# Gate and value products as 2x2 blocks with seven block products, and an MLP issued from a table of places

## The chip, the cores and the metric

One core of one Trainium2 chip runs the whole kernel. The metric is device time in microseconds, from launch to end; lower is better.

## The reference

Attention with hashed buckets feeds a gated layer, and that a second one. Cut to what is computed:

```
mask = q_bucket[..., :, None] == k_bucket[..., None, :]     # buckets: signs of q @ proj, k @ proj
scores = where(mask, (q @ k.T) / sqrt(64), -1e9)            # (2, 8, 768, 768)
x = softmax(scores) @ v                                     # -> (1536, 512)
x = (sigmoid(x @ moe_w_gate) * (x @ moe_w_val)) @ moe_w_out # 512 -> 1536 -> 512
h = x @ moe2_w_in                                           # 512 -> 2048
g = where(h >= 1, h, where(h <= -1, 0, (h + 1) ** 2 / 4))
out = g @ moe2_w_out                                        # 2048 -> 512
```

The MLP weights arrive as 64-bit floats, read as int64, and the kernel turns them into fp32 bit by bit.

## The kernel before

**Attention.** Two batches b with four pairs of heads p each give eight pairs q = 0 to 7, about 28 us each. A pair has 12 units (two heads, six row blocks of 128). Per unit TensorE writes the scores (`sc`), VectorE takes the row maximum, ScalarE the exponential `P`; TensorE transposes P into PSUM banks (`pt`), ScalarE copies the high half to f16 (`PT`, L345), VectorE the rest (L348), and TensorE multiplies by v's halves `vh` and `vl` into `O` (L387). GpSimd scales and splits v (L368, L371, L375), prepares q and k of the next pair (L209, L212, L215) and copies reciprocals (`rb`, L536). VectorE reduces v once a pair (L356). The order of all of it is written by hand: a table `AT` gives each step a place in units, `at` adds it to a list, and the sorted list is issued under `manual_schedule`, so that each engine runs its rows in that order.

**Precision.** Every fp32 operand of the MLP is split into a high and a low fp32r half (`split`, `split_w`, `conv_w` with `w_abs`, `w_clamp`, `w_low`, `w_sign` for the 64-bit weights), and a product is three matmuls, high by high, high by low, low by high (`mm3`, L125 to L130). The copies run on ScalarE, the differences on VectorE.

**Gate and value.** For each of 12 chunks of 128 output columns, each batch and each half n of its 768 tokens, `gate_val_n` multiplies four input chunks by the gate weights into one bank `pg`, takes tanh (L150), does the same with the value weights into `pv` and multiplies (L154). `first_weights` converts the first gate and value weights during pairs 1 to 3 in 10 steps, and `gv(0)`, `gv(1)` run the first two products at the end of the attention; `split_x` splits x on GpSimd in the last pair.

**The rest** is in the scheduler's own order from its own pool of eight PSUM banks: `out1` (12 weight chunks into eight accumulators, per batch), then `mlp2` (`act2` and the second output product).

## Time and profile before

| what | us |
| --- | --- |
| median of 3 runs | 825.41 (825.2 to 825.66) |
| span of the profiled execution | 821.7 |
| busy on PE, DVE, ACT, POOL | 804.5, 542.8, 462.3, 119.5 |
| stretch of the attention | 0 to about 249 |

The span runs from the first to the last instruction of the profiled execution on the core; a run's time holds in addition what lies ahead of and behind it. The profiled execution's own time is not recorded beside its span, so the span stands for it and the difference to the median is added. PE is TensorE (PEld its weight loads), DVE VectorE, ACT ScalarE, POOL GpSimd. An engine's busy time counts neither waits nor the issuing of transfers.

### The profile page before, as it was taken

Reading aid. Unit: us, or ns where it says so; the run is one execution under the profiler, and the core shown is the slowest. Engines: PE = TensorE matmul, PEld = TensorE weight load, DVE = VectorE, ACT = ScalarE, POOL = GpSimd, SP = SyncE. Lnnn points to the kernel's source line nnn. Section 1 sums busy time; section 2 is a strip of 40 time slices with the busy share of each in tenths; the row PEclk is TensorE's granted clock in tenths of the full one; section 3 lists DMA queues with packets and bytes.
Section 4 is the critical chain, followed back from the end, with each engine's and each line's share of the span. In section 5 each row is a group of like instructions: output and inputs, shape, how many; then the busy total and the mean of one; then the engine's idle time right before and its main releaser. Section 6 shows DMA issues by size and latency. Waiting matters only on the chain.

```text
span 821.7 us, 13003 instructions
## 1 busy us (share of the span) xinstructions
PE 804.5 (98%) x5098; PEld 736.1 (90%) x5098; DVE 542.8 (66%) x953; ACT 462.3 (56%) x903; POOL 119.5 (15%) x104
## 2 busy tenths in 40 slices
...
PEclk8999999999999999999999999999999999999999
...
GB/s 241 124 120 126 87 107 130 74 133 90 30 2 77 129 73 82 52 52 56 99 155 192 91 77 40 142 178 127 78 1 1 1 1 77 1 1 1 1 0 77
DMA packets 39709, 64.21 MB, mean 78 GB/s; under 512 B 5316, under 2 KB 28228, under 8 KB 39648
## 3 DMA queue, kind: packets, MB, share of 16 engines
...
## 4 chain that ended last, share of the span: by engine, by line
PE 89%; ACT 4%; DVE 3%; DMA 3%; issue 0%; SPq 0%; DVEq 0%
PE sc L301 6%; PE pt L336 6%; PE O L387 6%; PE p L128 5%; PE p L126 5%; PE p L127 5%; PE o L693 5%; PE o L694 5%; PE o L692 5%; PE pg L126 4%; PE pg L128 4%; PE pv L128 4%; PE y L128 4%; PE pg L127 4%; PE y L126 4%; PE pv L127 4%
## 5 line engine op out<-in xcount | busy, mean ns | idle before, releaser
L348 DVE SCALAR_TENSOR_TENSOR PT<-pt,PT 128x512 f16<-128x512 f32 x144 | 95.5, 685 | 19.7 <-ACT PT L345 17.9
L309 DVE TENSOR_REDUCE st<-sc 128x1 f32<-128x768 f32 x96 | 90.9, 948 | 5.4 <-PE sc L301 5.1
L313 ACT ACTIVATE P<-sc,st 128x768 f32<-128x768 f32 x96 | 86.9, 905 | 13.0 <-DVE st L309 12.8
L345 ACT ACTIVATE PT<-pt 128x512 f16<-128x512 f32 x144 | 81.7, 593 | 21.1 <-PE pt L336 20.6
L128 PE MATMUL p<-yh,wl_i 128*128 128x384 f32 x256 | 85.9, 336 | 0.0
L126 PE MATMUL p<-yh,wh_i 128*128 128x384 f32 x256 | 85.8, 335 | 0.0
L127 PE MATMUL p<-yl,wh_i 128*128 128x384 f32 x256 | 85.7, 335 | 0.0
L336 PE MATMUL pt<-ident,P 128*128 128x128 f32 x576 | 80.4, 277 | 4.8 <-DVE PT L348 3.5
L336 PEld LDWEIGHTS pt<-ident,P 128*128 128x128 f32 x576 | 66.0, 141 | 15.8 <-DVE PT L348 8.0
L694 PE MATMUL o<-wh_o,gl 128*128 128x512 f32 x192 | 75.3, 392 | 0.0
L693 PE MATMUL o<-wl_o,gh 128*128 128x512 f32 x192 | 75.2, 392 | 0.0
L692 PE MATMUL o<-wh_o,gh 128*128 128x512 f32 x192 | 74.7, 389 | 0.0
L676 DVE SCALAR_TENSOR_TENSOR g<-p,t 128x384 f32<-128x384 f32 x64 | 35.5, 555 | 48.3 <-ACT t L674 48.3
L154 DVE SCALAR_TENSOR_TENSOR h<-sg,pv 128x384 f32<-128x384 f32 x48 | 26.4, 551 | 50.4 <-PE pv L128 50.3
L150 ACT ACTIVATE sg<-pg 128x384 f32<-128x384 f32 x48 | 23.4, 488 | 63.4 <-PE pg L128 63.1
L673 ACT ACTIVATE t<-p,cst 128x384 f32<-128x384 f32 x64 | 36.7, 573 | 37.0 <-PE p L128 36.8
L677 ACT ACTIVATE gh<-g 128x384 fp32r<-128x384 f32 x64 | 33.6, 525 | 41.2 <-DVE g L676 41.1
L678 DVE TENSOR_TENSOR gl<-g,gh 128x384 fp32r<-128x384 f32 x64 | 35.7, 557 | 31.5 <-ACT gh L677 31.5
L387 PE MATMUL O<-PT,vh 128*64 128x256 f16 x576 | 54.8, 278 | 0.5 <-DVE xr L394 0.5
L126 PEld LDWEIGHTS p<-yh,wh_i 128*128 128x128 f32 x256 | 48.1, 188 | 1.1
L127 PEld LDWEIGHTS p<-yl,wh_i 128*128 128x128 f32 x256 | 48.1, 188 | 1.1
L116 DVE TENSOR_TENSOR wl_o<-w_o,wh_o 128x512 fp32r<-128x512 f32 x56 | 38.6, 689 | 15.0 <-ACT wh_o L115 15.0
(265 smaller groups left out, 2022.7 us busy)
## 6 DMA issues: line engine op xcount, KB each, us to landing
...
```

The costliest lines, as they stand in the source:

```text
L126: nc.tensor.matmul(ps, lhsT=wh, rhs=rh, start=first, stop=False)
L127: nc.tensor.matmul(ps, lhsT=wh, rhs=rl, start=False, stop=False)
L128: nc.tensor.matmul(ps, lhsT=wl, rhs=rh, start=False, stop=last)
L309: nc.vector.tensor_reduce(out=self.st[:, 0, self.c:self.c + 1], in_=self.sc[:, :, 0:HN], op=ALU.max, axis=AX.XY, negate=True)
L313: nc.scalar.activation(out=self.P, in_=self.sc[:, :, 0:HN], func=AF.Exp, bias=self.st[:, 0, self.c:self.c + 1], scale=1.0, accum_out=self. ...
L336: nc.tensor.transpose(self.ps[m][:, j, :], un[2 * self.n + e].P[:, a, c:c + 128], ident)
L345: nc.scalar.activation(out=self.part(0, m), in_=self.ps[m], func=AF.Copy, scale=PSCALE)
L348: nc.vector.scalar_tensor_tensor(out=self.part(1, m), in0=self.ps[m], scalar=PSCALE, in1=self.part(0, m), op0=ALU.mult, op1=ALU.subtract)
L387: nc.tensor.matmul(O_ps[r, 0:GN], lhsT=vv[m][:, e, i * D:(i + 1) * D], rhs=PT[:, l, e * NI + i, :], start=(s == 0), stop=(s == len(steps) ...
L692: nc.tensor.matmul(oacc[i], lhsT=gh[:, ts], rhs=wh, start=(fc == 0), stop=False)
L693: nc.tensor.matmul(oacc[i], lhsT=gh[:, ts], rhs=wl, start=False, stop=False)
L694: nc.tensor.matmul(oacc[i], lhsT=gl[:, ts], rhs=wh, start=False, stop=(fc == F2 - 1))
```

## The change

The weight chunks j and j + 6 form two rows of blocks, the four input chunks two block columns of two, and the two token halves the two block columns of x. In place of the eight block products, each of 2 x 3 matmuls, seven are made (`SEQ`), on sums and differences of blocks: S1 to S4 of the weights (`a_sum`), T1 to T4 of x (`b_sum`). A `Quad` does this for one chunk pair of gate or value (`t` = g0 to g5, v0 to v5) and one batch: 24 quads. A partial result that belongs to two outputs is copied from its PSUM bank to another by ScalarE (`seed`: a to b, b to c, b to d), and the next product adds to the copy; the one of bank e goes to SBUF (`keep5`) and VectorE adds it (`sum`). Banks b, c, d come in turn from the attention's pool, whose first four turns begin with a small matmul of zeros (`qbank`). The x sums and splits of batch 0 go to GpSimd in pairs 4 to 7, `first_weights` has 20 steps in pairs 1 to 5, and quad 0 (`tail`) runs at the end of the attention. From there on all MLP work is issued from one list of places under `manual_schedule`, with one PSUM pool throughout.

```diff
+    SEQ = (("A11", "B11", "a"), ("S1", "T1", "e"), ("S2", "T2", "b"), ("A12", "B21", "a"), ("S3", "T3", "b"), ("S4", "B22", "c"), ("A22", "T4", "d"))
...
-        nc.gpsimd.dma_start(code_f, code_d)
+        nc.sync.dma_start(code_f, code_d)
...
-        return keep.tile([128, S], F32R, tag="qk", bufs=16, name=name)
+        return keep.tile([128, S], dt, tag="qk", bufs=26, name=name)
...
+    def b_sum(eng, b, name, cs=slice(0, 2)):
+        x, y = {"T1": ("B12", "B11"), "T2": ("B22", "T1"), "T3": ("B22", "B12"), "T4": ("B21", "T2")}[name]
+        xsub(eng, BO[b][name][:, cs], b_src(b, x)[:, cs], b_src(b, y)[:, cs])
...
+    def a_conv(t, m):
+        if m < 2:
+            (w_range, w_shift)[m](WO[t]["wt"].bitcast(U32))
+        else:
+            w, (low, high) = a_half(t, m % 2)
+            w_low(w, low) if m < 4 else w_sign(w, high)
+
+    def a_sum(eng, t, m, q2=False):
...
+        o, x, y, op = ((s1, a21, a22, ALU.add), (s2, s1, a11, ALU.subtract), (s3, a11, a21, ALU.subtract), (s4, a12, s2, ALU.subtract))[m]
+        eng.tensor_tensor(out=o, in0=x, in1=y, op=op)
...
+        def keep5(self):
+            self.p5 = self.tmp(f"p5_{self.t}_{self.b}")
+            nc.scalar.activation(out=self.p5, in_=self.K["e"], func=AF.Copy)
+
+        def P(self, i):
+            an, bn, g = SEQ[i]
+            first = i < 2
+            ps = self.new(g) if first else self.K[g]
...
+            for c in range(2):
+                cs = slice(c * 128, (c + 1) * 128)
+                mm3(ps, wh[:, cs], wl[:, cs], rh[:, c], rl[:, c], first and c == 0, c == 1, skip_group_check=True)
+
+        def seed(self, m):
+            src = self.K["abb"[m]]
+            nc.scalar.activation(out=self.new("bcd"[m]), in_=src, func=AF.Copy)
...
+        def sum(self, g):
+
+            d = self.dst(g)
+            if g in "bc":
+                x = self.tmp(f"x{g}_{self.t}_{self.b}") if self.val else d
+                nc.vector.tensor_tensor(out=x, in0=self.K[g], in1=self.p5, op=ALU.add)
+            else:
+                x = self.K[g]
+            if self.val:
+                self.glu(d, x)
...
-    def gate_val_n(b, n, ws, hr, bank, sgt, nm, late=None):
...
+    def qbank(k, g):
+
+        if g in "ae":
...
+            return pairs[g][:, k % 2, 0:HN]
+        t = bank(f"q{g}_{k}", next(ring))[:, 0:HN]
+        if next(turn) < 4:
+            nc.tensor.matmul(t, lhsT=code[:, 0, 0, :], rhs=bt, start=True, stop=True, skip_group_check=True)
+        return t
...
             def first_weights():
...
+                for t in ("g0", "v0"):
+                    for h in range(2):
+                        a_abs(t, h)
+                        yield
+                    for m in range(6):
+                        a_conv(t, m)
+                        yield
+                    a_load({"g0": "v0", "v0": "g1"}[t])
+                    if t == "g0":
+                        for m in range(4):
+                            a_sum(nc.gpsimd, t, m)
+                        a_hi(t, "a")
+                        yield
+                        a_lo(t, "a")
+                        for m in range(2):
+                            a_hi(t, "s", m)
+                            yield
+                            a_lo(t, "s", m)
...
-            for i in range(10):
+            for i in range(20):
                 at(2.2 + 1.2 * (i % 4), 0, 1 + i // 4, next, fw, None)
...
+            x0 = ("T1", "hT1", "hB11", "lB11", "T2", "lT1", "hT2", "T4", "lT2", "T3", "hT3", "lT3", "hT4", "lT4", "hB21", "lB21", "hB22", "lB22")
...
+            place = [(4, 1.0 + 1.3 * i) for i in range(2)] + [(5, 2.0 + 2.1 * i) for i in range(4)] + [(6, 2.0 + 2.1 * i) for i in range(4)] + [(7, 0.5 + 1.2 * i) for i in range(8)]
+            for op, (q, t) in zip(x0, place):
+                at(t, 0, q, x_op, 0, op)
...
-            gv(1)
+            x_op(1, "T2", C1, V)
...
+            tail("P", 4)
...
+    for k in range(1, 2 * NT):
+        s0 = 7 * k
+        for i in range(7):
+            on(s0 + i, q_op, k, "P", i)
+        for m, d in enumerate((0.98, 2.98, 4.98)):
+            on(s0 + d, q_op, k, "seed", m)
+        on(s0 + 1.99, q_op, k, "keep5")
+        for g, d in (("a", 3.99), ("b", 4.99), ("c", 5.99), ("d", 6.99)):
+            on(s0 + d, q_op, k, "sum", g)
+            on(s0 + d + (0.5 if g in "bc" else 0.0), q_op, k, "act", g)
...
+        for m, d in enumerate((0.1, 0.9, 1.7, 2.4, 3.0, 3.6)):
+            on(base + d, a_conv, n, m)
...
+        for m, d in enumerate((8.05, 9.05)):
+            on(base + d, a_hi, n, "s", m, True)
+            on(base + d + 1.0, a_lo, n, "s", m, True)
...
-    for b in range(B):
-        out1(b)
-    for b in range(B):
-        mlp2(b)
+    with tc.manual_schedule():
+        for _, _, fn, args, kw in sorted(prog, key=lambda x: x[:2]):
+            fn(*args, **kw)
```

The order of ScalarE in the second quad (batch 1) of a gate chunk pair, here g4: `qb`, `qc`, `qd` are the seeds, `hs` the high halves of the next value weight sums, `wt` the weight after that, `h1` the gate, `qa` to `qe` the banks. After the change (rows that repeat a tanh left out):

```order
L257 ACTIVATE qb_17_5004<-qa_3678 128x384
L217 ACTIVATE hs_v4_5012<-ws_v4_4964 128x512
L243 ACTIVATE p5_g4_1_5014<-qe_3688 128x384
L217 ACTIVATE hs_v4_5012<-ws_v4_4964 128x512
L257 ACTIVATE qc_17_5025<-qb_17_5004 128x384
L140 ACTIVATE wt_g5_5034<-wr0_g5_4975 128x512
L260 ACTIVATE h1_4_4995<-qa_3678 128x384
L257 ACTIVATE qd_17_5043<-qb_17_5004 128x384
L140 ACTIVATE wt_g5_5034<-wr1_g5_4976 128x512
L260 ACTIVATE h1_4_4995<-qd_17_5043 128x384
```

Before, ScalarE at about the same chunk of the gate and value stretch, with `sg` the tanh of the gate and `wh`, `w` the weights:

```order
L150 ACTIVATE sg_0_6_0_4571<-pg_0_6_0_4558 128x384
L150 ACTIVATE sg_0_6_1_4600<-pg_0_6_1_4587 128x384
L150 ACTIVATE sg_1_6_0_4630<-pg_1_6_0_4617 128x384
L115 ACTIVATE wh_v_7_4695<-w_v_7_4687 128x512
L150 ACTIVATE sg_1_6_1_4659<-pg_1_6_1_4646 128x384
L93 ACTIVATE w_v_8_4829<-wr_v_8_4830 128x512
L115 ACTIVATE wh_g_8_4825<-w_g_8_4817 128x512
L93 ACTIVATE w_g_9_4959<-wr_g_9_4960 128x512
```

Four tanh copies a chunk and their weight copies have become seeds, copies of bank e and tanh with the weight copies in between, so that a seed now stands behind a 512-column copy.

The order of GpSimd in pair 5 (batch 1, head pair 1), from the copy of the first reciprocals `rb` on: `vr`, `vh`, `vl` are v and its halves, `n0` and `U1` the next pair's q and k. Before:

```order
L536 COPY rb_1_1_1_1_2535<-st_1_1_0_0_2309 128x256
L368 TENSOR_SCALAR vr_1_1_1952<-vr_1_1_1952,vm_1_1_2235 128x768
L371 CAST vh_1_1_2586<-vr_1_1_1952 128x768
L375 TENSOR_TENSOR vl_1_1_2629<-vr_1_1_1952,vh_1_1_2586 128x768
L209 TENSOR_SCALAR n0_1_3_2395<-n0_1_3_2395 128x768
L212 CAST U1_1_3_2662<-n1_1_3_2397 128x768
L536 COPY rb_1_1_1_3_2673<-st_1_1_0_2_2451 128x256
```

After, with `xT2` the sum T2 of x and `lT1` the low half of T1:

```order
L695 COPY rb_1_1_1_1_2560<-st_1_1_0_0_2327 128x256
L111 TENSOR_TENSOR xT2_0_2609<-xr_0_2_1409,xT1_0_1975 128x768
L537 TENSOR_SCALAR vr_1_1_1962<-vr_1_1_1962,vm_1_1_2253 128x768
L540 CAST vh_1_1_2618<-vr_1_1_1962 128x768
L111 TENSOR_TENSOR lT1_0_2654<-xT1_0_1975,hT1_0_2007 128x768
L544 TENSOR_TENSOR vl_1_1_2663<-vr_1_1_1962,vh_1_1_2618 128x768
L378 TENSOR_SCALAR n0_1_3_2413<-n0_1_3_2413 128x768
L381 CAST U1_1_3_2696<-n1_1_3_2415 128x768
L695 COPY rb_1_1_1_3_2707<-st_1_1_0_2_2472 128x256
```

Two operations on 768 columns now stand between `rb` and `vl`.

The order of VectorE in pair 3, where the maxima `st` and the low halves `PT` of the attention run: `wl_v` is the last step of the first weights before the change.

```order
L309 TENSOR_REDUCE st_0_3_0_0_1425<-sc_0_3_1_1_1521 128x1
L348 SCALAR_TENSOR_TENSOR PT_0_3_0_1529<-pt_18_0_1516,PT_0_3_0_1529 128x4x128
L309 TENSOR_REDUCE st_0_3_0_2_1570<-sc_0_3_0_2_1540 128x1
L348 SCALAR_TENSOR_TENSOR PT_0_3_0_1529<-pt_18_1_1555,PT_0_3_0_1529 128x4x128
L348 SCALAR_TENSOR_TENSOR PT_0_3_0_1529<-pt_19_1_1565,PT_0_3_0_1529 128x4x128
L424 TENSOR_TENSOR wl_v_0_1550<-w_v_0_1101,wh_v_0_1549 128x512
L309 TENSOR_REDUCE st_0_3_0_2_1570<-sc_0_3_1_2_1582 128x1
L348 SCALAR_TENSOR_TENSOR PT_0_3_0_1529<-pt_18_2_1589,PT_0_3_0_1529 128x4x128
L394 SCALAR_TENSOR_TENSOR xr_0_2_1416<-O_0_2_1_1438,rs_0_2_1_3_1423 128x256
L309 TENSOR_REDUCE st_0_3_0_2_1570<-sc_0_3_0_3_1610 128x1
L322 RECIPROCAL st_0_3_0_0_1425<-st_0_3_0_0_1425 128x4
L348 SCALAR_TENSOR_TENSOR PT_0_3_0_1529<-pt_19_0_1622,PT_0_3_0_1529 128x4x128
```

After, `la_g0` and `ls_g0` are the low halves of the gate weights' blocks and sums:

```order
L111 TENSOR_TENSOR la_g0_1597<-wt_g0_654,ha_g0_1552 128x768
L478 TENSOR_REDUCE st_0_3_0_2_1572<-sc_0_3_1_2_1584 128x1
L517 SCALAR_TENSOR_TENSOR PT_0_3_0_1522<-pt_18_2_1591,PT_0_3_0_1522 128x4x128
L565 SCALAR_TENSOR_TENSOR xr_0_2_1409<-O_0_2_1_1431,rs_0_2_1_3_1416 128x256
L111 TENSOR_TENSOR ls_g0_1627<-ws_g0_1547,hs_g0_1599 128x512
L478 TENSOR_REDUCE st_0_3_0_2_1572<-sc_0_3_0_3_1615 128x1
L491 RECIPROCAL st_0_3_0_0_1418<-st_0_3_0_0_1418 128x4
L517 SCALAR_TENSOR_TENSOR PT_0_3_0_1522<-pt_19_0_1630,PT_0_3_0_1522 128x4x128
L517 SCALAR_TENSOR_TENSOR PT_0_3_1_1655<-pt_20_0_1637,PT_0_3_1_1655 128x4x128
L478 TENSOR_REDUCE st_0_3_0_2_1572<-sc_0_3_1_3_1665 128x1
L517 SCALAR_TENSOR_TENSOR PT_0_3_1_1655<-pt_20_1_1670,PT_0_3_1_1655 128x4x128
L111 TENSOR_TENSOR ls_g0_1627<-ws_g0_1547,hs_g0_1599 128x512
```

Where one difference on 512 columns stood there are now three in this stretch, one of them on 768 columns.

## Rows read from the trace of the kernel before

**Rows 1.** The page: span, busy time by engine, granted clock in 40 slices.

```profile
span 821.7 us, 13003 instructions
PE 804.5 (98%) x5098; PEld 736.1 (90%) x5098; DVE 542.8 (66%) x953; ACT 462.3 (56%) x903; POOL 119.5 (15%) x104
PEclk8999999999999999999999999999999999999999
```

**Rows 2.** Windows: stretch, us; busy (instructions) PE, PEld, DVE, ACT, POOL; clock; DMA share; GB/s.

```profile
140.00:170.00 30.00, 30.00 (x267) 25.80 (x265) 26.52 (x45) 26.90 (x61) 13.11 (x11) 1.00 0.44 112
276.00:490.00 214.00, 214.00 (x1237) 214.00 (x1236) 125.57 (x230) 69.50 (x119) 0.00 (x0) 1.00 0.29 94
```

**Rows 3.** TensorE's waits: total us, times, longest us.

```profile
PE pt L336 <- DVE PT L348: 3.5, 7, 1.0
...
PE pg L126 <- DVE h L154: 0.7, 1, 0.7
```

**Rows 4.** Groups by line: count, busy us, mean ns, idle before and releaser.

```profile
L215 POOL TENSOR_TENSOR W<-n,U 128x768 fp32r<-128x768 f32 x14 | 25.3, 1822 | 0.7
L150 ACT ACTIVATE sg<-pg 128x384 f32<-128x384 f32 x48 | 23.4, 488 | 63.4 <-PE pg L128 63.1
L115 ACT ACTIVATE wh_g<-w_g 128x512 fp32r<-128x512 f32 x11 | 7.0, 633 | 1.5 <-DVE w_g L103 1.3
```

**Rows 5.** Timeline at the handover: start, us, operation, idle before.

```profile
248.81 0.33 PE L128 MATMUL pg<-x_3h,wl_g 128*128 128x384 f32 x1
249.19 0.49 ACT L150 ACTIVATE sg<-pg 128x384 f32<-128x384 f32 x1 [1.49 <-PE pg L128]
...
255.47 0.85 ACT L139 ACTIVATE x_3h<-xr 128x768 fp32r<-128x768 f32 x1 [3.60 <-DVE xr L394]
256.35 0.96 DVE L140 TENSOR_TENSOR x_3l<-xr,x_3h 128x768 fp32r<-128x768 f32 x1 [0.91 <-ACT x_3h L139]
...
259.37 0.56 DVE L154 SCALAR_TENSOR_TENSOR h<-sg,pv 128x384 f32<-128x384 f32 x1 [2.06 <-PE pv L128]
259.98 0.44 PE L126 MATMUL pg<-x_0h,wh_g 128*128 128x384 f32 x1 [0.72 <-DVE h L154]
```

**Rows 6.** Timeline of VectorE in pair 2.

```profile
84.84 0.68 DVE L424 TENSOR_TENSOR wl_g<-w_g,wh_g 128x512 fp32r<-128x512 f32 x1
85.44 0.42 DVE L96 TENSOR_SCALAR w_v<-w_v 128x512 f32<-128x512 f32 x1
```

**Rows 7.** Timeline of VectorE, the reduction once a pair, pairs 2 to 5.

```profile
67.24 0.94 DVE L356 TENSOR_REDUCE vm<-vr 128x1 f32<-128x768 f32 x1
...
97.53 0.94 DVE L356 TENSOR_REDUCE vm<-vr 128x1 f32<-128x768 f32 x1
...
125.98 0.94 DVE L356 TENSOR_REDUCE vm<-vr 128x1 f32<-128x768 f32 x1
...
153.94 0.94 DVE L356 TENSOR_REDUCE vm<-vr 128x1 f32<-128x768 f32 x1
```

**Rows 8.** Timeline of GpSimd in pair 5, and the first matmul on vl.

```profile
145.87 0.40 POOL L536 COPY rb<-st 128x256 f32<-128x256 f32 x1 [7.88 <-DVE st L322]
146.25 2.20 POOL L368 TENSOR_SCALAR vr<-vr,vm 128x768 f32<-128x768 f32 x1
148.52 0.82 POOL L371 CAST vh<-vr 128x768 f16<-128x768 f32 x1
149.43 1.65 POOL L375 TENSOR_TENSOR vl<-vr,vh 128x768 f16<-128x768 f32 x1
...
153.88 0.28 PE L387 MATMUL O<-PT,vl 128*64 128x256 f16 x2
```

**Rows 9.** Timeline of VectorE and GpSimd side by side in pair 1.

```profile
61.95 0.68 DVE L103 SCALAR_TENSOR_TENSOR w_g<-wr_g,w_g 128x512 uint32<-128x512 uint32 x1
62.17 1.14 POOL L371 CAST vh<-vr 128x768 f16<-128x768 f32 x1
```

**Rows 10.** Timeline at the start of the program.

```profile
6.82 0.41 DVE L447 CAST code<-code_f 56x512 bf16<-56x512 f32 x1
```

More of the change, by code (lines that the diff above doesn't have):

```diff
@@ L1 @@
 from contextlib import ExitStack
+from functools import cache
+from itertools import count, cycle
 import concourse.bass as bass
@@ L108, in conv_w @@
         w_abs(w, high)
-        w_clamp(w)
+        w_range(w)
+        w_shift(w)
         w_low(w, low)
@@ new lines, in on_split, with o_banks, o_mm @@
+    def on_split(t, dt, key, src, mk):
+        on(t, s_hi, key, src, mk)
+        on(t + dt, s_lo, key, src)
+    ACC, OA = {}, {}
+    def o_banks(b):
+        pair = [pairs[g] for g in "ae"]
+        single = [bank(f"y_{b}_{i}", g) for i, g in enumerate(("pv", "mm", "pt", "pt"))]
+        for c in range(KC):
+            ACC[b, c, 0], ACC[b, c, 1] = pair[c // 2][:, c % 2], single[c]
+    def o_mm(b, s, n):
+        if (b, 0, 0) not in ACC:
+            o_banks(b)
+        (wh, wl), (hh, hl) = WH["o", b, ORD[s]], WH["h", b, ORD[s]]
+        ns = slice(n * HN, (n + 1) * HN)
+        for c in range(KC):
+            cc = slice(c * 128, (c + 1) * 128)
+            mm3(ACC[b, c, n][:, 0:HN], wh[:, cc], wl[:, cc], hh[:, ns], hl[:, ns], s == 0, s == F1 - 1)
@@ new lines, in y_hi, with y_lo @@
+    def y_hi(b, c, n):
+        if b not in Y:
+            Y[b] = [tuple(qtile(f"y{g}_{b}_{c}") for g in "hl") for c in range(KC)]
+        ns = slice(n * HN, (n + 1) * HN)
+        nc.scalar.activation(out=Y[b][c][0][:, ns], in_=ACC[b, c, n][:, 0:HN], func=AF.Copy, scale=0.5)
+    def y_lo(b, c, n):
+        ns = slice(n * HN, (n + 1) * HN)
+        h, l = Y[b][c]
+        nc.vector.scalar_tensor_tensor(out=l[:, ns], in0=ACC[b, c, n][:, 0:HN], scalar=0.5, in1=f(h[:, ns]), op0=ALU.mult, op1=ALU.subtract)
@@ new lines, in z_mm @@
+    def z_mm(b, fc):
+        if b not in OA:
+            OA[b] = [pairs[g][:, i] for g in "ae" for i in range(2)] + [bank(f"o_{b}_{i}", "pt") for i in range(2)]
+        wh, wl = WH["z", b, fc]
+        gh, gl = GG[b, fc]
+        for i in range(NI):
+            ts = slice(i * 128, (i + 1) * 128)
+            nc.tensor.matmul(OA[b][i], lhsT=gh[:, ts], rhs=wh, start=(fc == 0), stop=False)
+            nc.tensor.matmul(OA[b][i], lhsT=gh[:, ts], rhs=wl, start=False, stop=False)
+            nc.tensor.matmul(OA[b][i], lhsT=gl[:, ts], rhs=wh, start=False, stop=(fc == F2 - 1))
```

547 lines of the change are left out of this document (368 added, 179 removed).

## Prediction

> **What bounds the kernel now.** I read the page first: one core, TensorE busy 804.5 of 821.7 us, VectorE 542.8, ScalarE 462.3, GpSimd 119.5, and the granted clock at full speed after the first slice, which is the higher level, 2.4 GHz [rows 1]. A second view, by stretch, says how it is full: from 276 to 490 us, where gate, value and the first output product run, PE is busy 214.00 of 214.00 us with 1237 matmuls, so one 128x384 matmul costs 214.00/1237 = 0.173 us. In the attention, 140 to 170 us, PE is busy too, but VectorE has 26.52 and ScalarE 26.90 of 30 us: three engines share that stretch [rows 2]. The list of TensorE's waits then holds little: seven waits on the copies of P's transposes, 3.5 us in all, and at the handover from attention to MLP one of 0.7 us on `h` [rows 3]. So in the MLP only fewer matmuls or a new stall move the end; in the attention, work added to any of three engines does.
>
> The profile's span is 821.7 us and the median of the runs 825.41, so about 3.7 us lie around the span; I sum on the span and add 3.7.
>
> **The change, part by part.**
>
> *Matmuls.* Before: 12 chunks x gate and value x 2 batches x 2 halves x 12 = 1152 matmuls. After: 24 quads x 7 block products x 2 x 3 = 1008. 144 fewer at 0.173 us [rows 2]: -24.9 us. `qbank` adds 4 matmuls in the first turns of the banks: +0.7.
>
> *Chain of a quad: the seeds.* Each product writes six matmuls into a bank, and three times a quad ScalarE copies a bank to another (`seed`), 72 copies in all. No row shows a copy from PSUM to PSUM; the nearest is tanh from PSUM, 488 ns for the same 128x384 [rows 4], and I take it, with 0.3 and 0.7 us as ends. Latencies: gate's last matmul starts at 248.81, its reader on ScalarE at 249.19, 0.38 later; VectorE's product ends at 259.93 and the waiting matmul starts at 259.98, 0.05 later [rows 5]. A seed's reader can thus start 0.38 + 0.49 + 0.05 = 0.92 us after the last matmul of the source started, and TensorE, one product of six in between, comes there after 7 x 0.173 = 1.21. Slack 0.29: where nothing stands ahead of it on ScalarE, a copy is free up to 0.78 us, at both ends above.
>
> What can make it late is the row order on ScalarE. In the part on the change, `qc_17` stands behind p5 and two 512-column copies. With the quad's first matmul at 0, product i (from 0) starts its last matmul at (6i + 5) x 0.173 and is readable 0.38 later, at 1.25 + 1.04i: qb 1.25 to 1.74, the first copy (0.63 [rows 4]) to 2.37, p5 to 2.86, the second copy to 3.49, qc to 3.98. The fifth product, which overwrites the source bank, comes at 24 x 0.173 = 4.15: slack 0.12 after the 0.05. It holds by little. Cost 0; the cover is the other product, and a copy of 0.7 us, 0.2 longer, passes the slack by 0.3 with qb's own lengthening, in some 11 such quads: +3 at that end. VectorE in a pair of value quads: weight work 1.7 + 2.7 + 1.6 + 2.3 us, sums and products 12 x 0.56 [rows 5], less the 0.08 by which neighbours overlap (a 0.68 us op at 84.84, the next at 85.44 [rows 6]): about 13 of 14.5 us. That engine is late next.
>
> *Handover.* The wait of 0.7 us on `h` goes with the code that had it [rows 3], and one of 0.5 us or so on the last `xr`. In their place the first quad runs between hand-placed sums and copies of x, and the next one finds ScalarE behind by its tanh and the copies of x, 0.85 us for 768 columns [rows 5]: I work out about 1.2 us ahead of its fifth product, 0.6 us in three smaller waits, and 0.2 at the start of the first output product. 2.0 - 1.2 = +0.8, with ends -1.2 (all hidden) and +4 (each seed of two quads late by one 0.85 us copy).
>
> *Attention, VectorE.* `first_weights` has 20 steps instead of 10, in five pairs instead of three. VectorE's part before is two weights of two ops of 0.42 and three of 0.68, 5.8 us [rows 6]. After: range and shift on 1024 columns 1.7 in pair 1, four half steps 2.76 in pair 2, the differences (0.96 + 2 x 0.69, by the rows for 768 and 512 columns [rows 5, 6]) 2.34 in pair 3, 2.4 and 2.07 for the value weight in pairs 4 and 5: 11.3 us, +5.5. What a us costs there is to be read: the once-a-pair reduction falls at 67.24, 97.53, 125.98 and 153.94, so the pairs last 30.29, 28.45 and 27.96 us [rows 7]. The first of these has 2.9 us of such work and is 2.3 longer than the third, which has none, the second 0.69 us and is 0.5 longer: 0.80 and 0.71 us for each, ScalarE's share included, and a little more against a still shorter pair. 5.5 x 0.71 to 0.84 is 3.9 to 4.6; not all of the new work lies in TensorE's tight places, so I take the lower end, +4.0. Ends: 0 (TensorE's full stretch hides it, since VectorE has 3.5 of 30 us free [rows 2]) and +7.7 (5.5 x 1.4, ScalarE's copies counted in series behind VectorE's work).
>
> *Attention, GpSimd.* The x sums and splits move into pairs 4 to 7. In pair 5 two of them now stand between `rb` and `vl` (the second piece of the order): 0.40 + 1.82 + 2.20 + 0.82 + 1.82 + 1.65 = 8.71 us, the subtractions at 1822 ns [rows 4]. Before, `rb` starts at 145.87 and the first matmul that needs `vl` at 153.88: 8.01 us [rows 8]. So `vl` is 0.7 us late, and again in pair 6. TensorE has other rows ahead in part: +1.0, ends 0 and +7.3 (if each of the two subtractions in both pairs is late in full, 4 x 1.82).
>
> *Ports.* Beside a VectorE op with two SBUF operands (61.95, 0.68 us) GpSimd's cast took 1.14 us, against 0.82 elsewhere [rows 8, 9]; VectorE's op was not longer. More GpSimd work meets more VectorE work: +0.5.
>
> A longer wait is the stronger form. The Trainium skill ("SBUF — State Buffer", "Who interferes with whom") states that a VectorE instruction with two SBUF inputs contends with a GpSimd instruction that reads SBUF, that in VectorE's 2-port modes one blocks fully, and that the one that issues first wins; the trace agrees for the half in which GpSimd waited (1.14 against 0.82), and shows no case the other way round. By the row the cost is GpSimd's 0.3 us a meeting; by the rule it can be VectorE's, and is a rival below.
>
> *The rest.* The code table's DMA goes from GpSimd's queue to SP's, behind the two loads of pair 0; its copy on VectorE starts only at 6.82 [rows 10], and pair 1's loads, 0.4 us later behind it, feed work of 30 us on: 0. Tile counts, and out1 and mlp2 by places instead of the scheduler's order, leave TensorE's rows as they were, and there the PE is without gaps [rows 2]: 0, with the ends +5 where a place is late, -1 for the handovers.
>
> Sum: -24.9 + 0.7 + 0.8 + 4.0 + 1.0 + 0.5 = -17.9; 821.7 - 17.9 = 803.8, and 3.7 around it: **807.5 us**.
>
> **Rivals.**
> - *Attention gives nothing back.* For it: VectorE has room in 30 us [rows 2]. Against: pair 2 grew by 2.3 us for 2.9 [rows 7]. 821.7 - 24.9 + 0.7 + 0.8 + 3.7 = 802.0.
> - *VectorE waits for GpSimd.* 11 ops on two SBUF operands and 4 on 1024 columns meet GpSimd's 1.82 us ops and wait for half of one on average, 0.91: 15 x 0.91 x 0.84 = 11.5 us. For it: GpSimd doubles its work there. Against: the one pair of rows shows GpSimd as the one that waits [rows 9]. 819.0 at worst.
> - *Places in the MLP are late.* A hand order with a slack of 0.12 us: if half of the 24 quads lose 0.4 to 1.2 us, that is 5 to 14 us, 812 to 822.
> - *Slower: the copies are the chain.* A copy from bank to bank takes c, and each of 72 makes TensorE wait c - 0.78. The gain of 17.9 is gone at 17.9/72 = 0.25, so it decides at c = 1.03 us, 2.1 times the row for tanh [rows 4]. For it: no row with both sides in PSUM. Against: ScalarE's rows from PSUM and from SBUF differ by columns, not by side. At c = 1.2: 837.8.
> - *Same:* between these, where the losses sum to the 24.9.
>
> **How the numbers follow.** Chances: forecast 0.58 (803 to 812), attention free 0.14, VectorE waiting 0.09, late places 0.10, slower 0.06, same 0.03. The bound of the last two is 0.2% of 825.4, 1.7 us, about what a measurement of this kernel can tell. The range from 800 to 818 holds the forecast, the free attention with 2 us for the handover's lower end, and most of the waiting and late cases; outside are the slower and same cases and the late places over 818. Faster 0.91, same 0.03, slower 0.06.
>
> **What would show it.** Right: some 140 fewer of PE's 5098 rows, PE fully busy with 0.173 us a matmul through gate and value, no wait on a seed in the list of PE's waits, seeds of 0.4 to 0.6 us; pairs 2 to 5 at 28.5 to 31 us by the same reduction, and a few us of waits on PT, P or O there; `vl` late by under 1 us in pairs 5 and 6. Wrong: waits of PE on `qb`, `qc` or `qd` summing over 3 us; seeds over 0.78 us; VectorE's 0.68 us ops at over 1 us beside GpSimd; pairs 4 to 7 unchanged from 27.96.

## The result, and the profile after

The changed kernel takes 812.12 us (811.33 to 812.29, four runs) against 825.53 for the kernel before beside it: a ratio of 0.9836, 95% interval 0.9822 to 0.985. That is 13.4 us less, where 17.9 were forecast; the time lies in the range from 800 to 818, 4.6 us over the value and 0.1 over the stretch of the forecast itself (803 to 812). One run of one experiment below stood at a granted clock of 0.848 throughout, took 866.87 us, and is left out of the comparisons.

The page of the changed kernel, its first lines:

```profile
span 809.6 us, 12950 instructions
PE 783.8 (97%) x4958; PEld 710.8 (88%) x4958; DVE 596.5 (74%) x1041; ACT 509.6 (63%) x1015; POOL 143.3 (18%) x127
PEclk8999999999999999999999999999999999999999
```

PE has 140 matmuls fewer and 20.7 us less of busy time; VectorE, ScalarE and GpSimd have more than in [rows 1]. The span fell by 12.1 us. The runs of this kernel show what lies around a span: 811.33 us for the span of 809.6, 812.29 for one of 810.5, so 1.8 us, and the same for the kernel before in later runs (826.3 for 824.5). The 3.7 us of the prediction were thus 1.8 around and, by this count, 1.9 by which the profiled execution of before was shorter than the median; the span's 12.1 us and the medians' 13.4 differ by that and by the 0.8 us that the change's profiled run lies under its median.

Two stretches of the changed kernel, by windows (us; PE, PEld, DVE, ACT, POOL busy): the end of the attention with the first two quads, and the other quads.

```profile
251.19:275.00 23.81, 21.82 (x162) 19.15 (x163) 15.34 (x27) 12.87 (x27) 7.69 (x9) 1.00 0.01 1
275.00:435.88 160.88, 160.52 (x927) 160.20 (x925) 126.94 (x232) 94.77 (x189) 0.00 (x0) 1.00 0.23 73
```

From the third quad on TensorE has no gap. From the first start to the last inside such a stretch a matmul takes 0.1733 us in both kernels, with the seeds in between as without them (160.88/927, or 0.1735, counts matmuls that the window's edges cut). Groups by line of the changed kernel: the seeds take 0.476 us, where 0.488 was taken from [rows 4].

```profile
L257 ACT ACTIVATE qc<-qb 128x384 f32<-128x384 f32 x24 | 11.4, 476 | 6.8 <-PE qb L294 5.7 <-PE qc L332 0.7
L257 ACT ACTIVATE qd<-qb 128x384 f32<-128x384 f32 x24 | 11.4, 476 | 20.4 <-PE qb L294 20.4
```

TensorE's waits in the changed kernel (total us, times, longest):

```profile
PE pt L505 <- DVE PT L517: 4.3, 8, 1.3
PE sc L470 <- DMA H<-U: 2.5, 2, 2.3
...
PE O L556 <- POOL vl L544: 1.6, 2, 1.0
PE qd L292 <- ACT qd L257: 1.3, 1, 1.3
...
PE sc L470 <- ACT rs L682: 1.0, 1, 1.0
PE p L292 <- DVE gg L951: 1.0, 2, 0.8
...
PE qb L292 <- ACT qc L257: 0.7, 1, 0.7
...
PE qa L293 <- DVE h_0l L111: 0.4, 1, 0.4
PE qe L292 <- DVE yl L933: 0.4, 1, 0.4
PE y L292 <- DVE h L263: 0.2, 1, 0.2
```

Against [rows 3] new names stand there: `vl`, the seeds `qc` and `qd` of one quad, and four at the starts of the MLP's stages (`h_0l`, `h`, `yl`, `gg`). The page's list names the engine that came last by the profile; behind `ACT rs` stands a transfer, as the run with fewer x operations shows. Next is the reduction on v once a pair in the changed kernel (VectorE's timeline), to be read against [rows 7] and two later ones of the kernel before, behind it:

```profile
96.81 0.94 DVE L525 TENSOR_REDUCE vm<-vr 128x1 f32<-128x768 f32 x1
...
127.10 0.94 DVE L525 TENSOR_REDUCE vm<-vr 128x1 f32<-128x768 f32 x1
...
156.06 0.94 DVE L525 TENSOR_REDUCE vm<-vr 128x1 f32<-128x768 f32 x1
...
185.72 0.94 DVE L525 TENSOR_REDUCE vm<-vr 128x1 f32<-128x768 f32 x1
...
215.88 0.94 DVE L525 TENSOR_REDUCE vm<-vr 128x1 f32<-128x768 f32 x1
```

```profile
181.81 0.94 DVE L356 TENSOR_REDUCE vm<-vr 128x1 f32<-128x768 f32 x1
...
209.68 0.94 DVE L356 TENSOR_REDUCE vm<-vr 128x1 f32<-128x768 f32 x1
```

The differences between neighbours are the pairs' lengths. Where an edit leaves a pair alone, pairs 1 to 5 repeat within 0.05 us from one profile to the next, so a difference of 0.2 us is readable there, while the runs' medians scatter by 1 us. Pair 6 does not repeat: with nothing changed in it, it lasts from 30.13 to 32.46 us (the change, code table, places, seed twice, eighth product). The traces say why: scores in this pair wait for the move of H from U, which lands 6.32 us into it in the change and 7.06 us into it in the run with each seed twice, and in that run the granted clock fell as well (see "x early"). The profiles that the experiments below left, in us (worked out from those starts; "first at" is the reduction of pair 1):

| kernel | first at | pair 1 | 2 | 3 | 4 | 5 | 6 |
| --- | --- | --- | --- | --- | --- | --- | --- |
| before | 37.95 | 29.29 | 30.29 | 28.45 | 27.96 | 27.87 | 27.87 |
| the change | 39.09 | 29.24 | 28.48 | 30.29 | 28.96 | 29.66 | 30.16 |
| code table | 41.21 | 29.25 | 28.46 | 30.28 | 28.96 | 29.66 | 30.63 |
| fewer x | 41.06 | 29.27 | 28.47 | 30.29 | 28.95 | 29.68 | 30.75 |
| fewer w | 40.36 | 29.24 | 28.50 | 30.31 | 28.32 | 27.89 | 30.10 |
| places | 39.75 | 29.24 | 28.49 | 30.28 | 28.92 | 29.66 | 30.13 |
| loads late | 40.61 | 29.24 | 28.46 | 31.44 | 28.96 | 29.66 | 29.06 |
| x early | 39.05 | 29.24 | 28.49 | 30.28 | 28.97 | 30.40 | 31.66 |
| steps apart | 39.59 | 29.26 | 28.48 | 30.30 | 28.94 | 28.99 | 29.26 |
| seed twice | 39.61 | 29.23 | 28.47 | 30.29 | 28.95 | 29.68 | 32.46 |
| eighth product | 38.69 | 29.23 | 28.46 | 30.28 | 28.93 | 29.67 | 30.19 |
| one load late | 39.05 | 29.24 | 28.46 | 30.30 | 28.95 | 29.68 | 29.07 |
| all together | 38.23 | 29.22 | 28.46 | 30.29 | 28.95 | 28.95 | 27.85 |

The account of the 12.1 us of span, then: the first reduction comes 1.14 later (start); from it to the last group of eight transposes of P (251.19 against 244.34 us) the attention takes 212.10 instead of 206.39, +5.71; from there to the end 558.41 instead of 577.36, -18.95.

### The profile page after: what moved, and what is told of

It is laid out like the page before. It is cut to its first block, busy times and chain, and to the rows that moved or that the text cites. A ratio compares the mean times of both kernels' runs of the same rounds, so it can differ in the third digit from the quotient of the medians.

```text
span 809.6 us, 12950 instructions
## 1 busy us (share of the span) xinstructions
PE 783.8 (97%) x4958; PEld 710.8 (88%) x4958; DVE 596.5 (74%) x1041; ACT 509.6 (63%) x1015; POOL 143.3 (18%) x127
## 4 chain that ended last, share of the span: by engine, by line
PE 82%; ACT 7%; DVE 6%; DMA 3%; issue 1%; POOL 0%; SPq 0%; POOLq 0%; ACTq 0%
PE sc L470 6%; PE p L292 5%; PE p L294 5%; PE p L293 5%; PE O L556 5%; PE pt L505 5%; PE qa L292 3%; PE qa L294 3%; PE qa L293 3%; ACT P L482 2%; PE y L292 2%; PE y L293 2%; PE y L294 2%; PE qb L292 2%; PE qb L294 2%; PE qb L293 2%
## 5 line engine op out<-in xcount | busy, mean ns | idle before, releaser
L951 DVE SCALAR_TENSOR_TENSOR gg<-p,t 128x384 f32<-128x384 f32 x64 | 35.6, 556 | 91.4 <-ACT t L948 91.4
L292 PE MATMUL p<-yh,whl_i 128*128 128x384 f32 x256 | 86.1, 336 | 1.0 <-DVE gg L951 1.0
L294 PE MATMUL p<-yh,whl_i 128*128 128x384 f32 x256 | 86.0, 336 | 0.0
L293 PE MATMUL p<-yl,whl_i 128*128 128x384 f32 x256 | 85.8, 335 | 0.0
L292 PEld LDWEIGHTS p<-yh,whl_i 128*128 128x128 f32 x256 | 48.1, 188 | 2.8 <-DVE gg L951 1.6
L293 PEld LDWEIGHTS p<-yl,whl_i 128*128 128x128 f32 x256 | 48.1, 188 | 1.2
L294 PEld LDWEIGHTS p<-yh,whl_i 128*128 128x128 f32 x256 | 48.1, 188 | 0.0
L556 PEld LDWEIGHTS <-vh 128*64 128x64 f16 x576 | 30.7, 109 | 11.2 <-issue 10.7
L556 PE MATMUL O<-PT,vl 128*64 128x256 f16 x288 | 34.2, 273 | 1.6 <-POOL vl L544 1.6
L948 ACT ACTIVATE t<-t 128x384 f32<-128x384 f32 x64 | 33.6, 525 | 1.8
L470 PE MATMUL sc<-H,H 128*128 128x384 f32 x96 | 30.0, 394 | 4.3 <-DMA H<-U 2.5
L470 PE MATMUL sc<-N,N 128*128 128x384 f32 x96 | 29.1, 385 | 0.0
```

What stands on the lines that cost most here:

```text
L292: nc.tensor.matmul(ps, lhsT=wh, rhs=rh, start=first, stop=False, **kw)
L293: nc.tensor.matmul(ps, lhsT=wh, rhs=rl, start=False, stop=False, **kw)
L294: nc.tensor.matmul(ps, lhsT=wl, rhs=rh, start=False, stop=last, **kw)
L470: nc.tensor.matmul(self.sc[:, n, 0:HN], lhsT=M[:, ts], rhs=K[:, n * HN:(n + 1) * HN], start=s0, stop=not s0)
L556: nc.tensor.matmul(O_ps[r, 0:GN], lhsT=vv[m][:, e, i * D:(i + 1) * D], rhs=PT[:, l, e * NI + i, :], start=(s == 0), stop=(s == len(steps) ...
L951: nc.vector.scalar_tensor_tensor(out=g, in0=PS[k], scalar=1.0, in1=TT[k], op0=ALU.max, op1=ALU.min)
```

## The experiments

The theory after the result: the matmuls' 24.9 us came; the attention gives back what was forecast, but through GpSimd and the loads rather than VectorE's own work; the rest went into hand-set places at the starts of the MLP's stages. The rival is the prediction's own account, VectorE's work at 0.71 to 0.84 us for each, and nothing at the places.

**The code table's load** on ScalarE's queue.

```diff
-        nc.sync.dma_start(code_f, code_d)
+        nc.scalar.dma_start(code_f, code_d)
```

> Only the code table's load is moved, from SP's queue to ScalarE's, ahead of ident. If its place ahead of pair 1's loads on SP's queue is what makes the first scores wait (2.28 us on the move of H, 1.83 on that of U, where before they waited 0.90 and 1.43), the first once-a-pair reduction of pair 1 falls back from 39.09 to about 38 us and the time from 812.1 to 811.0. Rival: the start is late for another reason (the tiles B from another pool, the smaller descriptor scratch); then it stays at 39.1 and 812.1.

812.30 us (ratio 0.9834, 0.9814 to 0.9853): no change. The first scores came 0.8 us earlier, but the reduction of pair 1 at 41.21, later than in any other run: the theory of the start fell. Over the profiles of the changed kernel and its variants it lies between 38.23 and 41.21 with nearly the same code ahead of it. What differs is when a 512-byte move of v's maxima arrives, which VectorE waits for: issued at 17.61 and read at 24.82 us here, issued at 19.56 and read at 23.05 in the change.

**Fewer x operations** on GpSimd.

```diff
+                if op not in ("T2", "lT1", "hT2", "T4", "lT2", "T3", "hT3", "lT3"):
+                    at(t, 0, q, x_op, 0, op)
```

> Eight operations of GpSimd on x are left out in pairs 5 and 6 (T1's operands stand in for T2, T3, T4). If GpSimd is what lengthens these pairs (late vl, VectorE held behind GpSimd), pair 6 goes from 30.2 to about 28.3 us and pair 5, which keeps two of them, from 29.7 to 28.5: about -3, 809. Rival, VectorE's own work on the first weights: pair 5 stays at 29.5, pair 6 has none of it and its 2.3 us are then something else: -1 at most, 811.

812.56 (0.9843, 0.9828 to 0.9857). The waits on `vl` were gone, and pair 6 lasted 30.75 all the same: TensorE then waited 2.77 us ahead of its scores. On the pairs the rival was right: pair 5 stayed at 29.68 (VectorE's step was held there as in the change, 2.08 us at 171), and pair 6 is held by something else. The trace names it: the move of H from U landed at 194.63 and the scores started at 194.72, as in the change at 192.04 and 192.12.

**Fewer steps on the value weight.** VectorE's six conversion operations for it in pairs 4 and 5 are left out.

```diff
                     for m in range(6):
-                        a_conv(t, m)
+                        if t == "g0":
+                            a_conv(t, m)
```

> The six steps of VectorE on the first value weight in pairs 4 and 5 are left out (4.5 us of work); its copies by ScalarE and its loads stay. By the prediction's price of 0.71 to 0.84 us for each: -3.2 to -3.8, 808.6. Rival, that VectorE's work is nearly hidden and only the op held behind GpSimd in pair 5 counts: the wait of 1.30 us at 172 us goes, pair 4 from 29.0 to 28.5 and pair 5 from 29.7 to 28.4: -1.3 to -2, 810.4.

809.42 (0.9804, 0.9789 to 0.9819). That lies between the two sides. Pair 4 fell by 0.64 and pair 5 by 1.77, for three steps of 0.68 us in each, 2.05 and 2.04 us in the change's trace where 4.5 in all were assumed; pair 6 stayed at 30.1, so it isn't VectorE's work on this weight that holds it. The held step in pair 5 costs 0.7 by the run with the steps apart, below, which leaves 1.1: (0.64 + 1.1)/4.09 is 0.43 us for each us, about half of the prediction's price.

**Places in the MLP.**

```diff
-    on(8.6, a_hi, "v0", "a", 0, True)
-    on(8.7, a_lo, "v0", "a", 0, True)
+    on(10.3, a_hi, "v0", "a", 0, True)
+    on(11.2, a_lo, "v0", "a", 0, True)
...
-        on(10.05 + m, a_hi, "v0", "s", m, True)
+        on(12.0 + 0.6 * m, a_hi, "v0", "s", m, True)
...
-    on_h(0, 0, end - 3.0)
-    on_h(0, 1, end - 1.8)
+    on_h(0, 0, end - 4.2)
+    on_h(0, 1, end - 2.7)
...
-                on_h(nb, ns, t0 + 0.7)
+                on_h(nb, ns, t0 + (-0.6 if (nb, ns) == (1, 1) else 0.7))
...
-        on_conv(w_conv, nconv, end + 0.5 + 5.0 * (nconv - F1 + 1))
+        on_conv(w_conv, nconv, end + 0.5 + 5.0 * (nconv - F1 + 1) + (2.2 if nconv < F1 else 0.0))
```

> Places in the table only: the value weight's high copies behind the seeds of the second quad, h's splits ahead of the first output product earlier, one split at the change of batch earlier, one weight conversion at the start of mlp2 later. If the waits at the handovers (0.66, 1.30, 0.36, 0.19, 0.35, 0.75, 0.22 us, 3.8 in all) come from rows queued ahead on ScalarE and VectorE, they go: about -3.5, 808.6. Rival: what is moved is late in its turn and gives new waits of the same size: over 811.

808.57 (0.9794, 0.978 to 0.9809): -3.5 against the change. By its trace 2.8 of them lie behind the last transposes of P (555.6 against 558.4 us to the end); the rest is within the medians' scatter. Of the waits behind the attention two are left in the list of this kernel, one of them new (the first seed of the third quad behind the weight copies that were moved).

```profile
PE qb L292 <- ACT qb L257: 1.1, 1, 1.1
...
PE p L292 <- DVE gg L951: 0.2, 1, 0.2
```

**Two loads late.** The loads of the first value and the second gate weight leave the steps.

```diff
-                    a_load({"g0": "v0", "v0": "g1"}[t])
...
+            at(9.0, 0, 2, a_load, "v0")
+            at(9.0, 0, 6, a_load, "g1")
```

> The loads of the first value weight and of the second gate weight (1 MB each) leave the first weights' steps, where they stand ahead of the next pair's moves of H, N, U and W on SP's queue in pairs 3 and 5, and are issued in pairs 2 and 6 behind those moves. If the 2.3 us of pair 6 come from these moves landing late (H from U is issued at 189.32 us where before it was issued at 183.13), the wait of 0.98 us ahead of the scores at 192 us goes, pair 6 falls from 30.2 to 28.5 or less; pair 3, 1.8 longer than before, goes to 29: -2 to -3, 809.5. Rival, that ScalarE's copy named in that wait is late by itself or by VectorE: pair 6 stays over 29.8, the time at 812.

813.31 (0.985, 0.9827 to 0.9873): no gain in sum, but the table above splits it. Pair 6 fell by 1.1, pair 3 grew by 1.15: there the value weight's load now stood ahead of the 512-byte move of v's maxima, and VectorE waited 1.18 us for it. What pair 6 waits for is on SP's queue. The changed kernel:

```profile
182.76 0.54 SPq L186 DMA_DIRECT2D wr_g<-in_moe_w_gate_dram  x1
183.39 0.50 SPq L188 DMA_DIRECT2D wr_g<-in_moe_w_gate_dram  x1
183.94 0.51 SPq L189 DMA_DIRECT2D wr_g<-in_moe_w_gate_dram  x1
184.50 0.47 SPq L448 DMA_DIRECT2D N<-H  x1
189.32 0.47 SPq L448 DMA_DIRECT2D H<-U  x1
```

The move of N from H is issued behind 1 MB of weight. It landed at 189.26, and the next one, which waits for that, was issued 4.82 us after it; with the load away (this kernel), 2.52 us:

```profile
187.07 0.46 SPq L448 DMA_DIRECT2D N<-H  x1
189.59 0.46 SPq L448 DMA_DIRECT2D H<-U  x1
```

**One load late**, the gate weight's alone.

```diff
-                    a_load({"g0": "v0", "v0": "g1"}[t])
+                    if t == "g0":
+                        a_load("v0")
...
+            at(9.0, 0, 6, a_load, "g1")
```

> Only the second gate weight's load is moved, out of pair 5 to the end of pair 6; the first value weight's stays in pair 3. If in the run with both loads moved the loss in pair 3 (31.4 instead of 30.3 us) was the value weight's and the gain in pair 6 (29.1 instead of 30.2) the gate weight's, then here pair 3 lasts 30.3, pair 6 29.1, with no wait ahead of the scores at 192 us, and the time is 811.0. Rival, that the second wait of pair 6 on vl takes the place: pair 6 at 30, 812.

811.15 (0.9831, 0.9809 to 0.9853), pair 3 at 30.30, pair 6 at 29.07, no wait ahead of those scores: as expected in each number. So this load costs 1.1 us (29.06 and 29.07 with the load away; 30.10 or more in all runs that left it there but the one with the steps apart, below), and `vl` does not take its place.

**The first load late.** The first gate weight's load goes to the end of pair 0.

```diff
-            a_load("g0")
...
+            at(9.0, 0, 0, a_load, "g0")
```

> Only the load of the first gate weight (1 MB) is moved, from the start to the end of pair 0. The start of the profiled runs so far scattered by 3 us (the reduction of pair 1 at 38 to 41.2 us), by the 512-byte move of v's maxima, which takes 3.5 to 7.2 us behind that load. If the load is what it waits behind, the reduction of pair 1 falls to 36 to 38 us, and the time by 1.5 to 3, 809.8, with less scatter. Rival, the move is late by itself or behind the loads of q and k: 812, and the same scatter.

811.19, 812.72 and 815.56 us in three runs (ratio 0.985, 0.9824 to 0.9876): no gain, and no less scatter. There is no trace to compare, so why the move of v's maxima comes late in some runs is left open.

**x early.** Four x operations ahead of the first `rb`.

```diff
-            place = [(4, 1.0 + 1.3 * i) for i in range(2)] + [(5, 2.0 + 2.1 * i) for i in range(4)] + [(6, 2.0 + 2.1 * i) for i in range(4)] + [(7, 0.5 + 1.2 * i) for i in range(8)]
+            place = [(4, 1.0 + 1.3 * i) for i in range(2)] + [(5, 2.0 + 0.7 * i) for i in range(4)] + [(6, 2.0 + 0.7 * i) for i in range(4)] + [(7, 0.5 + 1.2 * i) for i in range(8)]
```

> Four operations of GpSimd on x are moved ahead of the first rb in pairs 5 and 6, so that vl isn't behind them: the waits on vl, 1.02 and 0.55 us, go. In pair 5 two of them then run beside VectorE's two steps on the signs, which read two SBUF operands. If whichever of the two engines came first holds the other (VectorE's step of 0.68 us took 2.08 beside such an operation), one or two of these steps take 1.2 to 2.4 us, and pair 5 keeps a wait on PT: 811.5. Rival, only GpSimd waits for VectorE: no step over 0.8 us there, and -1.5: 810.5.

813.80 (0.9858, 0.9843 to 0.9872), 1.7 over the change, with intervals that overlap. The waits on `vl` went, and pair 5 grew by 0.74, pair 6 by 1.5. VectorE and GpSimd side by side in pair 5 of this kernel:

```profile
168.96 1.83 POOL L111 TENSOR_TENSOR lB<-xr,hB 128x768 fp32r<-128x768 f32 x1
169.26 2.08 DVE L149 SCALAR_TENSOR_TENSOR wt_v<-wr_v,wt_v 128x512 uint32<-128x512 uint32 x1
170.75 2.26 POOL L111 TENSOR_TENSOR xT<-xr,xT 128x768 f32<-128x768 f32 x1
172.97 1.83 POOL L111 TENSOR_TENSOR lT<-xT,hT 128x768 fp32r<-128x768 f32 x1
173.93 1.42 DVE L152 SCALAR_TENSOR_TENSOR wt_v<-wr_v,wt_v 128x512 uint32<-128x512 uint32 x1
```

Both operations of VectorE, 0.68 us elsewhere, began inside one of GpSimd's and ended 0.55 us after it; GpSimd's next one, begun inside VectorE's, took 2.26 instead of 1.83. The engine that came first held the other.

Pair 6 grew for another reason. Its scores wait for the move of H as before and start 6.31 us into the pair, in the change 6.41; but TensorE, not held by `vl`, came earlier and waited 2.07 us. Behind that wait the granted clock fell from 2.4 to 1.2 GHz for 3.41 us (windows of this kernel, then a like stretch of the change):

```profile
193.39:196.80 3.41, 3.41 (x22) 2.52 (x20) 2.27 (x4) 1.85 (x3) 0.00 (x0) 0.50 0.15 34
```

```profile
192.90:196.31 3.41, 3.41 (x33) 2.94 (x31) 3.00 (x8) 2.19 (x5) 1.57 (x1) 1.00 0.12 26
```

At the lower level TensorE did 22 matmuls where the change did 33. In the run with each seed twice the same followed a wait of 1.75 us, in the run with fewer x operations it did not follow one of 2.77, so what decides it is open. The 1.5 us of pair 6 thus say nothing against the order of GpSimd's work.

**Steps apart.** Steps of the value weight to where GpSimd is idle (three places change, the fourth stays at 5.8).

```diff
-                at(2.2 + 1.2 * (i % 4), 0, 1 + i // 4, next, fw, None)
+                at((3.6, 4.4, 5.1, 5.8)[i - 16] if i > 15 else 2.2 + 1.2 * (i % 4), 0, 1 + i // 4, next, fw, None)
```

> Only the four steps of the first value weight in pair 5 move, to where GpSimd is idle (from about 171 to 178 us). If VectorE's step of 2.08 us at 169 us was held by GpSimd's operation that began before it, no step there takes over 0.8 us, the wait of 1.30 us on PT at 172 us is gone, and pair 5 lasts 28.4 instead of 29.7: -1.3 at the end of the pair, and less of it at the end where pair 6 waits for its moves: 811.2. Rival, the step is long because it reads one of the raw words late: it stays at 2 us wherever it stands.

810.54 (0.9816, 0.98 to 0.9832). The same two operations in this kernel:

```profile
169.51 1.84 POOL L111 TENSOR_TENSOR lB<-xr,hB 128x768 fp32r<-128x768 f32 x1
173.18 0.68 DVE L149 SCALAR_TENSOR_TENSOR wt_v<-wr_v,wt_v 128x512 uint32<-128x512 uint32 x1
```

The wait of 1.30 us on PT was gone; pair 5 fell by 0.67 (a smaller wait of 0.48 us came in), and pair 6 by 0.9: its move of H was issued 2.90 us into it instead of 3.60. From the first reduction to the last transposes the attention took 210.59 us, 1.5 less than in the change.

**A seed twice.**

```diff
-            nc.scalar.activation(out=self.new("bcd"[m]), in_=src, func=AF.Copy)
+            dst = self.new("bcd"[m])
+            for _ in range(2):
+                nc.scalar.activation(out=dst, in_=src, func=AF.Copy)
```

> Each seed is made twice, one copy behind the other (0.475 us each, about 0.87 with the overlap). By the slack worked out in the prediction (a copy is free up to 0.78 us, in the quads with weight copies ahead of it up to some 0.6) TensorE waits 0.1 to 0.3 us at most of the 72 seeds: +7 to +20, 819 to 832, and the list of waits shows qb, qc, qd. Rival, that the slack is larger because something else runs between (ScalarE is 66% busy there): +0 to +2.

834.88 (1.0114, 1.0095 to 1.0134): +22.8, 2.9 over the upper end of what was expected. The timeline of this kernel at one seed:

```profile
299.08 0.98 ACT L259 ACTIVATE qc<-qb 128x384 f32<-128x384 f32 x2 [0.85 <-PE qb L296]
...
299.75 0.34 PE L296 MATMUL qa<-hB,la_g 128*128 128x384 f32 x1
300.12 0.44 PE L294 MATMUL qb<-hT,hs_g 128*128 128x384 f32 x1
...
300.40 0.34 PE L295 MATMUL qb<-lT,hs_g 128*128 128x384 f32 x1
```

The two copies take 0.98 us, without overlap. By the prediction's formula the reader is late by 0.38 + 0.98 + 0.05 - 1.21 = 0.20; it starts 0.37 us after its neighbour instead of 0.173, late by 0.20. The second matmul follows after 0.28 instead of 0.17, another 0.11, which the formula doesn't have. 72 times 0.30 is 21.6 of the 22.8 us; by the trace 22.65 lie behind the last transposes of P. Of the sides the main one was right, at its upper end for every seed.

**An eighth product.**

```diff
+            if i == 3:
+                for c in range(2):
+                    cs = slice(c * 128, (c + 1) * 128)
+                    mm3(ps, wh[:, cs], wl[:, cs], rh[:, c], rl[:, c], False, c == 1, skip_group_check=True)
```

> In each of the 24 quads the fourth product is added a second time, 144 matmuls more, so that the matmuls are as many as before the change and the rest is the change's; the product counted twice makes another sum. If the 144 matmuls are worth their 24.9 us in full, the time is 812.1 + 24.9 = 837, less what the longer quad takes off the waits behind the seeds (0.5 at most). Rival, that ScalarE or VectorE already share the bound of the quads: the eighth product is partly hidden, 825 to 832.

836.57 (1.014, 1.0118 to 1.0162): +24.45, 0.170 us for each of the 144 matmuls. By the trace the part behind the last transposes is 24.0 us longer, and the wait of 0.66 us in the second quad, worth 0.9 with its late second matmul, is gone: together 24.9. Nothing of them is hidden, and with as many matmuls as before the rest of the change would have cost 11 us.

**All together**: the gate weight's load, x early with the steps at 4.9 to 6.2, the places with the value weight's copies and differences moved once more and one conversion of the next weight later, and the last batch's output in a tile for each row block.

```diff
+                at((4.9, 5.5, 6.1, 6.2)[i - 16] if i > 15 else 2.2 + 1.2 * (i % 4), 0, 1 + i // 4, next, fw, None)
...
+        on(12.0 + 0.3 * m, a_hi, "v0", "s", m, True)
+        on(13.05 + 0.05 * m, a_lo, "v0", "s", m, True)
...
+                part(nc.scalar, nc.scalar.copy, "")
+            else:
+                part(nc.sync, nc.vector.tensor_copy, "")
```

> What the runs point to, together: the second gate weight's load behind pair 6's moves, four x operations ahead of the first rb with VectorE's steps behind them, the places at the start of the MLP and of its stages, the last batch's output in a tile for each row block with the odd ones on ScalarE's queue. Terms: places -3.5 and another -0.8 at the first seed of the second pair, pair 6 -1.1, vl -1.5, the held step -1.3, the end -0.8, which makes -9: 803. Rival, the waits in pairs 5 and 6 take each other's place, as in the run with fewer x operations: -5.5, 806.5.

805.31 (0.9753, 0.9729 to 0.9777), 20.4 under the kernel before and 6.8 under the change, nearer to the rival's 806.5 than to 803. Pair 6 is back at 27.85, `vl` has no wait, and the waits behind the attention are 0.31 and 0.24 us. The end gained 0.34 of the 0.8 expected: from the start of the last matmul to the end of the span are 5.37 us here, 5.71 in the change. By its trace 3.4 us of the gain over the change lie in the attention, 3.6 behind it and 0.9 in the start, which scatters.

## Why the prediction was right, and where its sum was off

**Matmuls (-24.9, +0.7 for four more).** Right: 24.45 by the eighth product, 24.9 by its trace.

**Seeds (0).** Right as a mechanism and in size, the seeds being 0.476 us: no wait from the third quad on, where the least slack is 0.20 us (a seed that ends 0.25 us ahead of its reader, less the 0.05) and 0.12 was worked out. A copy 0.5 us longer costs 0.30 each. The slower rival's price of c - 0.78 is confirmed but for the 0.11 that a late matmul adds, so its point of decision would be 0.92 us instead of 1.03.

**Handover (+0.8).** Right in mechanism and size. Beyond 0.1733 us for each matmul of gate and value, TensorE spends 9.27 us from the last transposes to 276 us in the change, 7.67 from there to 275 us before: +1.6, of which 0.7 are the four matmuls of zeros, so +0.9. ScalarE's queue held two seeds of the second quad, by 0.66 and 1.30 us; the wait of 0.72 at 259.98 [rows 5] and another of 0.52 went. For the first of the two, tanh and copies of x stand ahead on ScalarE, as forecast, and a copy of the value weight. The second wait has another start, which the prediction didn't have: GpSimd holds VectorE, whose sums `ws` of the value weight come late, ScalarE sits idle for 1.15 us in front of its copy of them, and `qd` stands behind:

```profile
268.85 1.20 POOL L111 TENSOR_TENSOR lT<-xt,hT 128x384 fp32r<-128x384 f32 x1
269.10 1.36 DVE L111 TENSOR_TENSOR lT<-xt,hT 128x384 fp32r<-128x384 f32 x1
...
271.29 0.63 ACT L217 ACTIVATE hs_v<-ws_v 128x512 fp32r<-128x512 f32 x1 [1.15 <-DVE ws_v L210]
...
272.38 0.48 ACT L260 ACTIVATE h<-qa 128x384 f32<-128x384 f32 x1
...
272.75 0.63 ACT L217 ACTIVATE hs_v<-ws_v 128x512 fp32r<-128x512 f32 x1
273.27 0.49 ACT L257 ACTIVATE qd<-qb 128x384 f32<-128x384 f32 x1
273.91 0.41 PE L292 MATMUL qd<-hT,ha_g 128*128 128x384 f32 x1 [1.30 <-ACT qd L257]
```

The run with other places moved these copies behind the seeds, and both waits went; no run took away the hold alone.

**The rest (0, ends +5 and -1).** This is the step that failed: places at the starts of out1 and mlp2 were costed at nothing because TensorE's rows there stay as they were. Before, no matmul there started over 0.06 us late; by the table the first rows of each stage stand behind VectorE's splits, sums and weight steps, and lose 3.2 us with the second matmuls (five waits of 0.19 to 0.75 us in the list). In the run with other places 2.1 of the 3.2 are gone. The end is 0.9 us longer (5.71 against 4.79 us from the last matmul's start). The range's +5 held it.

**Attention (VectorE +4.0, GpSimd +1.0, ports +0.5).** The sum of 5.5 stands beside 5.71, but by luck, with errors of opposite sign. By the table pairs 1 to 3 last as long together as before (88.01 and 88.03 us), pair 4 is 1.00 longer, pair 5 1.79, pair 6 2.29, and the way from there to the last transposes 0.65. VectorE's term was too large: the work was 10.5 us and not 11.3 (a range or shift step on 1024 columns takes 0.68 to 0.70 us), it cost nothing in sum in pairs 1 to 3, and about 0.4 us for each where it was taken away in pairs 4 and 5. GpSimd's was too small: `vl` is late by 1.02 and 0.55 where 0.7 twice was worked out, 1.6 us against the +1.0 taken. The hold of VectorE gave the wait of 1.30 us on PT in pair 5 and costs 0.7. A term of 1.1 was missing: the weight's load ahead of pair 6's moves. The prediction listed `first_weights`' copies and differences and left out the loads that its steps issue.

VectorE waiting for GpSimd, the rival at 0.09, was thus true in kind. Of the fifteen operations that it counted two were held, by 0.48 us at 121.33 and 1.40 at 169.29, and two more at the handover, by 0.38 and 0.81. The prediction put it low because it saw no such case in the trace of before. That trace does show one, at the start, on an operation of VectorE that takes 0.94 us two rows on:

```profile
5.27 0.82 POOL L256 CAST N<-U 64x768 fp32r<-64x768 f32 x1 [2.74 <-ACT U L205]
...
5.30 1.60 DVE L206 SCALAR_TENSOR_TENSOR W<-n,U 128x768 fp32r<-128x768 f32 x1
...
7.16 0.94 DVE L206 SCALAR_TENSOR_TENSOR W<-n,U 128x768 fp32r<-128x768 f32 x1
```

The Trainium skill ("SBUF — State Buffer", "Who interferes with whom") says that issue order decides which of the two is blocked; these runs agree, with 2.08 and 1.42 us for VectorE and 2.26 for GpSimd.

**The signs.** Of those for being right, the count of matmuls, their 0.173 us, the seeds' length and the pairs' lengths came; two seeds of one quad were waited for (2.0 us, under the 3 of the other list), and `vl` was late by 1.02 once. Of those for being wrong one came, VectorE's 0.68 us operations at over 1 us beside GpSimd.

**Attention free** (802.0) did not happen. The time is over the value by the places and the longer end (4.1 us) and the start (1.1, which scatters); that it still lay in the range is owed to the +5 kept for the places, and to the attention's errors cancelling.
